# Early loads in the order of their use: a transformer block on one core, with its weight, halo and store transfers regrouped

## The chip, the cores and the metric

The kernel runs on one core of a Trainium2 chip. The metric is device time in microseconds of one execution. The core has a matrix engine (TensorE, PE in the profile; its weight loads are listed as PEld), a vector engine (VectorE, DVE), a scalar engine (ScalarE, ACT), GpSimd (POOL) and SyncE (SP), which here does nothing but issue DMA transfers. The transfers of all issuers run on the core's 16 DMA engines; q1 is the queue of SP, q10 that of ACT.

## The reference

The input `x` has 2048 tokens of D = 576 features, in bf16. Two branches are computed from the same layer norm of `x` and added to it:

```
xn  = layernorm(x)
A:  q, k, v = xn @ wqkv                  (32 heads of 18)
    each token attends to itself and 7 earlier ones, 2 apart
    (positions s, s-2, ... s-14; those before 0 are masked)
    a   = softmax(q.k / sqrt(18)) . v,   then a @ wo
B:  f   = (silu(xn @ w_gate) * (xn @ w_up)) @ w_down      (4608 hidden)
out = x + A + B
```

## The kernel before

**Layout.** Token s = 16 p + r stands in partition p as row r, so there are 16 "rows" of 128 tokens. The attention needs rows up to 14 back. A ring of 18 rows (`Kr`, `Vr`) holds the 14 last rows of the partition before (the halo, which must be moved across partitions by DMA) and four rows of its own.

**Buffers that serve twice.** `wd`, the down-projection weights, is 9 chunks of 576 KB. Before they are loaded, its first 62% hold the raw rows of x (`xc_b`, chunks 0 to 3) and the normalized rows (`xn_b`, in chunks 4 to 6). Chunks 7 and 8 hold nothing. `hT`, the hidden activations, holds in its front the QKV weights and in its second half four staging buffers (`stage`), two for keys and two for values, of four rows each. A group c of rows (4c to 4c + 3) uses key and value buffers 0 and 1 when c is even, 2 and 3 when c is odd, so row 8 writes over group 0 and row 12 over group 1.

**QKV stage, rows 0 to 15 in order (lines 456 to 481).** For each row r, PE computes q, k and v (`p_row0`, `p_row`, L268): five slices kt of the contraction, 432 columns at a time in four PSUM banks, 36 matmuls on half the partitions each from row 1 on. ACT copies the banks out (`p_evac`): q to `QO`, k and v to staging. Ahead of PE run layer norm on DVE and ACT (`ln_*`, `pair_stats`, `pair_apply`) and the transposition of the normalized row: on PE for rows 0 to 4 (L232, L250), by DMA from SP for rows 5 to 15 (`transp_dma`, L258). For rows 2 to 4 the PE transposes are put between the matmuls of the row before (`between`). PE's first matmuls are warm-up on zeros (`warm_pe`).

**Halos and stores (`halo`, L328).** Once group c is in staging, SP issues for keys and then for values: the halo in two pieces (112 and 15 partitions, L334 and L335), and the group itself, into the ring for group 0 (L337) or to DRAM for groups 1 to 3 (`kv_d`, L339), from where `ring_load` fetches it later.

**Feed-forward, four passes of four rows (line 521 on).** Each pass goes over 9 chunks of 512 hidden columns. `g_pair` makes gate and up with PE (L506), `g_evac` the product on ACT (L517, L518) and DVE (L519). Gate/up weights (`gu`, four transfers a chunk) have two slots: chunk i + 2 can be loaded into a slot once PE has read chunk i. Chunks 0 and 1 are loaded within the QKV stage (at rows 9 and 12). During pass 0, each chunk also loads one or two chunks of `wd` (order 8, 0, 1, ... 7) and a part of `wo`. Then the down and output projections follow for each row (L552, L555).

**Attention on DVE (`chain`).** Its steps stand in a list from which fixed points of the program take steps (`dve.take` in the QKV stage, `dve.pump` after each activation). Keys are multiplied at L364; offset 7 and 6 need halo group 1, 5 and 4 also group 2, 3 to 1 group 3.

**What sets the order.** Each engine, SP too, works through its own list strictly in the order of the program text; the schedule is written by hand. SP's list is one queue: a transfer is issued only after those in front of it have been, and one that waits holds all behind it. Transfers take eight completion semaphores in turn, so each also waits for the eighth one before it to have landed.

Of the kernel before, what the change touches and what calls it, by code (L numbers as in the profile page):

```python
# [29 lines left out]
R = 16  # L30
# [40 lines left out]
def kernel(  # L71
# [11 lines left out]
    nc = tc.nc  # L83
# [58 lines left out]
    def load_w(eng, kt):  # L142
        if kt < 4:
            eng.dma_start(wqkv[:, kt, :], A_wqkv[kt * P:(kt + 1) * P, :])
        else:
            for i in range(2):
                eng.dma_start(wqkvr[64 * i:64 * i + 64, :], A_wqkv[4 * P:D, 2 * G * i:2 * G * (i + 1)])

    nc.sync.dma_start(xc_b[0][0:64, 0, :], x_v[0:64, 0, :])
    nc.scalar.dma_start(xc_b[0][64:128, 0, :], x_v[64:128, 0, :])  # L150
    load_w(nc.scalar, 0)
    nc.sync.dma_start(xc_b[0][:, 1, :], x_v[:, 1, :])
    load_w(nc.scalar, 2)
    make_identity(nc, ident[:])
    load_w(nc.sync, 1)
    nc.sync.dma_start(xc_b[0][:, 2, :], x_v[:, 2, :])
    load_w(nc.sync, 3)
    load_w(nc.sync, 4)
    nc.sync.dma_start(xc_b[0][:, 3, :], x_v[:, 3, :])
    for c in range(1, 4):  # L160
        nc.sync.dma_start(xc_b[c], x_v[:, 4 * c:4 * c + 4, :])
    nc.scalar.activation(warm[:], eps_t[:], ACT.Sqrt)
# [38 lines left out]
    def ln_stats(r, n=1):  # L201
        c, j = divmod(r, 4)
        xc, xn, mv, rstd = ln[c]
        for i in range(j, j + n):
            stats = lns.tile([P, 2, 6], f32, name="stats")
            for k in range(2):
                nc.vector.bn_stats(stats[:, k, :], xc[:, i, k * HALF:(k + 1) * HALF])  # L207
            nc.vector.bn_aggr(mv[:, i, :], stats[:].rearrange("p c s -> p (c s)"))

    def ln_sqrt(r, n=1):  # L210
        c, j = divmod(r, 4)
        xc, xn, mv, rstd = ln[c]
        nc.scalar.activation(rstd[:, j:j + n], mv[:, j:j + n, 1], ACT.Sqrt, bias=eps_t[:], scale=1.0)

    def ln_recip(r, n=1):
        c, j = divmod(r, 4)
        rstd = ln[c][3]
        nc.vector.reciprocal(rstd[:, j:j + n], rstd[:, j:j + n])

    def ln_apply(r, lo=0, hi=D):  # L220
        c, j = divmod(r, 4)
        xc, xn, mv, rstd = ln[c]
        nc.vector.tensor_scalar(xn[:, j, lo:hi], xc[:, j, lo:hi], mv[:, j, 0:1], rstd[:, j:j + 1],
                                op0=ALU.subtract, op1=ALU.mult)
        if hi == D:
            nc.vector.tensor_copy(xn[:, j, D:DPAD], xn[:, j, 512:D])
# [64 lines left out]
    def p_row(r, between=None):  # L291


        t = [None] * NG
        fence = {}
        for swap in range(2):
            for i in range(2):
                kts = (0, 1, 2, 3) if swap else (0, 4, 1, 2, 3)
                for kt in kts:
                    for half in range(2):  # L300
                        g = i + 2 * (half ^ swap)
                        if t[g] is None:
                            t[g] = new_ps("qkv_ps")
                        mm = p_mm(t, g, kt, half, r, swap == 0 and kt == 0, swap == 1 and kt == 3)
                        if swap == 0 and kt == 3 and half == 1:
                            fence[i] = fence_after(mm)
                        if swap and kt == 0 and half == 0:
                            fence_before(mm, fence[i])
                if swap and i == 0 and between is not None:
                    between()  # L310
        return t

    def p_evac(r, t):
        c, j = divmod(r, 4)
        ks, vs = stage[2 * c % 4], stage[(2 * c + 1) % 4]
        vdst = vs[:, j, :].rearrange("p (d h) -> p d h", h=H)

        def v_copy(lo, n, src):
            nc.scalar.copy(vdst[:, :, lo:lo + n], src.rearrange("p (h d) -> p d h", d=DH))  # L319

        nc.scalar.copy(QO[:, r, 0:G], t[0][:, 0:G])  # L321
        nc.scalar.copy(ks[:, j, HALF:D], t[2][:, 0:HALF])
        v_copy(0, 8, t[2][:, HALF:G])
        nc.scalar.copy(QO[:, r, G:D], t[1][:, 0:D - G])
        nc.scalar.copy(ks[:, j, 0:HALF], t[1][:, D - G:G])
        v_copy(8, 24, t[3][:, 0:G])

    def halo(m, c):  # L328
        ring = Kr if m == 1 else Vr
        st = stage[(2 * c + m - 1) % 4]  # L330
        lo = 2 if c == 0 else 0
        s0 = 4 * c - 2 + lo
        n = 4 - lo
        nc.sync.dma_start(ring[1:113, s0:s0 + n, :], st[0:112, lo:4, :])  # L334
        nc.sync.dma_start(ring[113:128, s0:s0 + n, :], st[112:127, lo:4, :])  # L335
        if c == 0:
            nc.sync.dma_start(ring[:, HALO:HALO + RT, :], st)  # L337
        else:
            nc.sync.dma_start(kv_d[m - 1, c - 1], st.rearrange("p r d -> p (r d)"))  # L339

    def ring_load(m, tt):
        ring = Kr if m == 1 else Vr
# [85 lines left out]
    def first():  # L428
        pt = new_pt()
        transp_pe(1, range(KT), pt)  # L430
        ln_stats(2)
        copy_pt(nc.scalar.copy, 1, range(3), pt)
        copy_pt(nc.vector.tensor_copy, 1, range(3, KT), pt[:, 3 * P:])
        ln_sqrt(2)
        ln_recip(2)
        ln_apply(2)

    warm_pe(11)
    ln_open(0)
    ln_stats(0)  # L440
    ln_sqrt(0)
# [14 lines left out]
    for r in range(R):  # L456
        if r == 0:
            t = p_row0(first)
        else:
            t = p_row(r, (lambda: transp_halves(r + 1)) if r <= 3 else None)  # L460
        if r == 1:
            ln_recip(3)
            ln_apply(3)
        p_evac(r, t)
        if r == 0:
            ln_stats(3)
            ln_sqrt(3)
        if 2 <= r <= 7:
            pair_apply(2 * r)
        if 1 <= r <= 6:  # L470
            pair_stats(2 * r + 2)
        if r and r % 4 == 0 or r == R - 1:
            c = r // 4 - (r < R - 1)
            halo(1, c)
            halo(2, c)
        if r in (9, 12):
            load_gu((r - 9) // 3)
        if r == 7:
            chain(0)
        if r in (7, 8, 12):  # L480
            dve.take(3 if r == 7 else 6)


    wd_order = [8, 0, 1, 2, 3, 4, 5, 6, 7]
    wo_order = list(range(DH))
    ring_ps = {}

# [33 lines left out]
    for tt in range(NTT):  # L521
        for ch in range(NCH):
            it = tt * NCH + ch
            for p in range(2):
                g_pair(tt, ch, p)
                for j in (2 * p, 2 * p + 1):
                    g_evac(ch, j)
                    dve.pump(1.4)
                if 1 <= it <= 4:
                    for _ in range(3 if it <= 1 else 2):  # L530
                        load_wo(wo_order.pop(0))
            if ch == NCH - 1:
                dve.drain(lambda: chains[0] > tt)
                for r in range(RT * tt, RT * tt + RT):
                    nc.sync.dma_start_transpose(oT[:, :, r * P:(r + 1) * P], QO_t[:, r * D:r * D + KT * P])
            if it + NSLOT < NTT * NCH:
                load_gu(it + NSLOT)
            if tt == 0:
                for _ in range(2 if ch in (5, 6) else 1):
                    if wd_order:  # L540
                        load_wd(wd_order.pop(0))
            if ch == 4:
                nc.sync.dma_start(xr[:], x_v[:, RT * tt:RT * tt + RT, :])
            if ch == 1 and tt < NTT - 1:
                chain(tt + 1)
        for sub in range(RT):
            r = RT * tt + sub
            t = [new_ps("d_ps") for h in range(2)]
            for h in range(2):
                cols = slice(h * HALF, (h + 1) * HALF)  # L550
                for f in range(NF):
                    nc.tensor.matmul(t[h][:, 0:HALF], hT[:, f, sub * P:(sub + 1) * P], wd[:, f, cols],  # L552
                                     start=(f == 0), stop=False)
                for k in range(KT):
                    nc.tensor.matmul(t[h][:, 0:HALF], oT[:, k, r * P:(r + 1) * P], wo[:, k, cols],  # L555
                                     start=False, stop=(k == KT - 1))
            dve.pump(8.5)
            ot = tmp.tile([P, D], bf16, name="ot", tag="ot", bufs=3)
            for h in range(2):
                cols = slice(h * HALF, (h + 1) * HALF)  # L560
                nc.vector.tensor_tensor(ot[:, cols], t[h][:, 0:HALF], xr[:, sub, cols], op=ALU.add)  # L561
                if r == R - 1:
                    nc.sync.dma_start(out_v[:, r, cols], ot[:, cols])
            if r < R - 1:
                nc.sync.dma_start(out_v[:, r, :], ot[:])
# [30 lines left out]
```

## Time and profile before

| | us |
|---|---|
| median of 3 runs (lowest, highest) | 514.27 (512.72, 516.37) |
| profiled execution, its own time | 515.68 |
| its span | 513.8 |
| PE busy | 503.4 (98%) |
| DVE, ACT busy | 327.3, 199.8 |
| feed-forward pass 0, first to last matmul of L506 | 62.60 to 138.36 |
| pass 1, the same | 178.64 to 248.68 |

The times in views are microseconds from the start of the span. A wait "X <- Y" says that X stood idle until Y ended. Matmuls are pipelined and their ends are modelled, so "busy" for PE includes the time in which a matmul ran slowly; the granted clock (1.00 is full speed) stands in a column of its own. A DMA share of 1.00 means that all 16 DMA engines are moving bytes; it can come out a little above. The time to landing of a transfer is counted from its issue, and holds the time in which it stood behind others.

### The profile page before, as it was taken

To read this page: it belongs to the slowest core of one execution; us is meant where nothing else is said; L and a number is where in the kernel's file an instruction comes from. 1 tells how busy PE (TensorE), PEld (TensorE's weight loads), DVE (VectorE), ACT (ScalarE), POOL (GpSimd) and SP (SyncE) were. 2 spreads that over 40 slices of the span, in tenths; PEclk is the share of its full clock that TensorE was granted. 3 is DMA by queue.
4 is the path that set the end of the run, shared out by engine and by line. 5 is a ranking of instruction groups with operands and counts; after the bars stand their busy time and mean duration, and the time that the engine had idled before them with its cause. 6 is when DMAs were issued, how large, how long until landed. Compare 5 with 4: busy or idle time off the path is not lost.

```text
span 513.8 us, 10678 instructions
## 1 busy us (share of the span) xinstructions
PE 503.4 (98%) x4516; PEld 294.4 (57%) x4516; DVE 327.3 (64%) x472; ACT 199.8 (39%) x415; POOL 2.5 (0%) x10
## 2 busy tenths in 40 slices
PE   7999989999999999999999999999999999999997
PEld 3655755444577744444677644444777444445775
DVE  5784569798999969999797129996990122112010
ACT  3656644755500055554400255458000355454000
POOL 1000000000000000000000000000000000000000
PEclk9999989999999999999999999999999999999999
DMA  8379998889751036474622053654500145542000
GB/s 273 96 188 196 307 312 260 291 274 295 233 138 59 11 105 192 132 231 138 168 83 70 11 154 124 213 162 134 144 13 23 60 138 185 174 150 40 25 13 24
DMA packets 75711, 75.01 MB, mean 146 GB/s; under 512 B 21948, under 2 KB 71448, under 8 KB 75664
## 3 DMA queue, kind: packets, MB, share of 16 engines
q1 hardware_dynamic: 75232, 73.35, 47.5%
q10 hardware_dynamic: 368, 0.96, 0.6%
q8 instruction: 35, 0.57, 0.5%
q14 instruction: 12, 0.10, 0.1%
q0 software_dynamic: 64, 0.03, 0.0%
HBM read 58.69 MB, written 5.90 MB: 126 GB/s over the span
## 4 chain that ended last, share of the span: by engine, by line
PE 80%; DMA 6%; ACT 2%; SPq 1%; DVE 1%; issue 1%; ACTq 0%
PE g_ps L506 50%; PE d_ps L552 27%; PE d_ps L555 4%; DMA gu<-in_B_w_gate_dram 2%; DMA gu<-in_B_w_up_dram 2%; DMA kv_d<-hT 1%; SPq L335 1%; DMA xnT<-wd 0%; DVE ssum L390 0%; ACT uc L518 0%; ACT hT L319 0%; DVE hT L519 0%; SPq L178 0%; ACT L389 0%; DVE PP L396 0%
## 5 line engine op out<-in xcount | busy, mean ns | idle before, releaser
L506 PE MATMUL g_ps<-xnT,gu 64*128 64x512 bf16 x2592 | 283.2, 377 | 2.8 <-DMA gu<-in_B_w_up_dram 2.8
L506 PEld LDWEIGHTS <-gu 64*128 64x128 bf16 x2592 | 132.2, 94 | 152.8 <-DMA gu<-in_B_w_up_dram 4.2
L517 ACT ACTIVATE sg<-g_ps 128x512 bf16<-128x512 f32 x144 | 87.4, 607 | 163.6 <-PE g_ps L506 163.6
L552 PE MATMUL d_ps<-wd,hT 128*128 128x288 bf16 x1152 | 146.6, 286 | 0.5 <-DVE hT L519 0.5
L552 PEld LDWEIGHTS <-hT 128*128 128x128 bf16 x1152 | 112.4, 98 | 30.7 <-issue 1.3
L519 DVE TENSOR_TENSOR hT<-sg,uc 128x512 bf16<-128x512 bf16 x144 | 60.2, 418 | 93.3 <-ACT uc L518 93.3
L518 ACT CAST uc<-g_ps 128x512 bf16<-128x512 f32 x144 | 85.5, 594 | 0.0
L369 DVE TENSOR_REDUCE PP<-PP 128x64 f32<-128x1152 bf16 x64 | 85.0, 1346 | 0.5
L268 PE MATMUL qkv_ps<-hT,xnT 64*128 64x432 bf16 (+1 forms) x560 | 54.2, 343 | 1.6 <-DMA hT<-in_A_wqkv_dram 1.5
L364 DVE TENSOR_TENSOR PP<-QO,Kr 128x2304 bf16<-128x2304 bf16 (+1 forms) x35 | 43.5, 1249 | 16.5 <-DMA Kr<-hT 16.2
L561 DVE TENSOR_TENSOR ot<-d_ps,xr 128x288 bf16<-128x288 f32 x32 | 13.8, 452 | 58.7 <-PE d_ps L555 58.6
L268 PEld LDWEIGHTS <-xnT 64*128 64x128 bf16 (+1 forms) x560 | 31.5, 94 | 22.8 <-issue 2.4
L396 DVE TENSOR_TENSOR PP<-Vr,A 128x2304 bf16<-128x2304 bf16 (+1 forms) x35 | 43.3, 1250 | 0.5
L401 DVE TENSOR_TENSOR PP<-PP 128x2304 bf16<-128x2304 bf16 x24 | 32.5, 1354 | 0.4
L517 ACT ACT_TABLE_LOAD x5 | 6.4, 1283 | 52.4 <-PE g_ps L506 52.3
L555 PE MATMUL d_ps<-wo,xnT 128*128 128x288 bf16 x160 | 24.8, 286 | 0.0
L555 PEld LDWEIGHTS <-xnT 128*128 128x128 bf16 x160 | 15.6, 98 | 4.0
L319 ACT CAST hT<-qkv_ps 128x144 bf16<-128x144 f32 (+1 forms) x32 | 14.0, 439 | 2.7 <-DMA kv_d<-hT 2.7
L207 DVE BATCH_NORM_STATS2 stats<-wd 128x6 f32<-128x288 bf16 x32 | 12.7, 440 | 3.5 <-DMA wd<-in_A_x_dram 3.5
L389 ACT ACTIVATE PP<-PP 128x1024 f32<-128x1024 f32 x4 | 4.2, 1057 | 27.5 <-DVE PP L385 27.5
L321 ACT CAST QO<-qkv_ps 128x432 bf16<-128x432 f32 x16 | 8.3, 517 | 7.6 <-PE qkv_ps L268 7.5
L390 DVE TENSOR_REDUCE ssum<-PP 128x128 f32<-128x1024 f32 x4 | 7.6, 1912 | 2.3 <-ACT PP L389 2.3
(39 smaller groups left out, 89.3 us busy)
## 6 DMA issues: line engine op xcount, KB each, us to landing
gu<-in_B_w_gate_dram SPq DMA_DIRECT2D x36, 512.0 KB, 3.8
gu<-in_B_w_up_dram SPq DMA_DIRECT2D x36, 512.0 KB, 5.0
wd<-in_B_w_down_dram SPq DMA_DIRECT2D x9, 576.0 KB, 6.2
kv_d<-hT SPq DMA_DIRECT2D x6, 576.0 KB, 7.1
gu<-in_B_w_gate_dram SPq DMA_DIRECT2D x36, 64.0 KB, 4.7
gu<-in_B_w_up_dram SPq DMA_DIRECT2D x36, 64.0 KB, 4.4
xr<-in_A_x_dram SPq DMA_DIRECT2D x4, 576.0 KB, 5.7
out_dram<-ot SPq DMA_DIRECT2D x15, 144.0 KB, 1.8
```

Source lines behind the costliest of these rows:

```text
L268: return nc.tensor.matmul(t[g][:, 0:G], xnT[rows, kt, r * P:(r + 1) * P], w_at(g, kt, rows), start=start, stop=stop)
L319: nc.scalar.copy(vdst[:, :, lo:lo + n], src.rearrange("p (h d) -> p d h", d=DH))
L364: nc.vector.tensor_tensor(prod[:, a:b], QO[:, RT * tt + a:RT * tt + b, :], Kr[:, s:s + b - a, :], op=ALU.mult)
L369: nc.vector.tensor_reduce(L[:, w, rs], prod[:, rs].rearrange("p r (h d) -> p r h d", d=DH), axis=AX.X, op=ALU.add)
L396: nc.vector.tensor_tensor(dst[:, a:b], Vr[:, s:s + b - a, :].rearrange("p r (d h) -> p r d h", h=H), A[:, w, a:b].unsqueeze(2).to_broadcas ...
L401: nc.vector.tensor_tensor(dst, acc, pv, op=ALU.add)
L506: mm = nc.tensor.matmul(ring_ps[j][b][:], gu[rows, slot, k, fc], xnT[rows, kt, tok], start=(swap == 0 and kt == 0), stop=(swap == 1 and kt ...
L517: nc.scalar.activation(sg[:], t[0][:], ACT.Silu)
L518: nc.scalar.copy(uc[:], t[1][:])
L519: nc.vector.tensor_tensor(hT[:, ch * FC + j, :], sg[:], uc[:], op=ALU.mult)
L552: nc.tensor.matmul(t[h][:, 0:HALF], hT[:, f, sub * P:(sub + 1) * P], wd[:, f, cols], start=(f == 0), stop=False)
L555: nc.tensor.matmul(t[h][:, 0:HALF], oT[:, k, r * P:(r + 1) * P], wo[:, k, cols], start=False, stop=(k == KT - 1))
```

## The change

All is a matter of order; no arithmetic is changed.

- The QKV weight slices, two of which ACT issued, all go through SP, between the rows of x, in the order kt 0, kt 1, x row 1, kt 2, kt 3, x row 2, kt 4, x row 3.
- Gate/up chunk 0 and down chunk 7 are loaded at row 0, down chunk 8 at row 2, gate/up chunk 1 at row 8 ahead of the halos of group 1. Down chunks 0 to 6 follow in pass 0, one with each chunk.
- The key halo of group 0 goes out after row 4, the value halo after row 6. For groups 1 to 3, both halos go ahead of both stores, which are a function of their own (`store`). The stores of group 3 wait until after chunk 0 of pass 0, behind the load of gate/up chunk 2.
- The PE transposes of rows 2 to 4 are placed four matmuls earlier (after kt 1 of the second half's first bank pair, instead of after its kt 3).
- Layer norm of row 2: statistics after the copies of row 1's transposes, its square root on ACT after the first copy of row 0. Two more warm-up matmuls (13 for 11).

On SP the first rows of the list are now: x row 0 (half), the weights and x rows as above, x groups 1 to 3, gate/up chunk 0, down chunk 7, transpose of row 5, down chunk 8, transposes of rows 6 to 9, key halo of group 0, transposes of rows 10 to 13, value halo of group 0, transposes of rows 14 and 15, gate/up chunk 1, halos of group 1, stores of group 1, halos and stores of group 2, halos of group 3, gate/up chunk 2, stores of group 3, down chunk 0.

```diff
+    def load_x(j):
+        nc.sync.dma_start(xc_b[0][:, j, :], x_v[:, j, :])
+
     nc.sync.dma_start(xc_b[0][0:64, 0, :], x_v[0:64, 0, :])
     nc.scalar.dma_start(xc_b[0][64:128, 0, :], x_v[64:128, 0, :])
-    load_w(nc.scalar, 0)
-    nc.sync.dma_start(xc_b[0][:, 1, :], x_v[:, 1, :])
-    load_w(nc.scalar, 2)
     make_identity(nc, ident[:])
+    load_w(nc.sync, 0)
     load_w(nc.sync, 1)
-    nc.sync.dma_start(xc_b[0][:, 2, :], x_v[:, 2, :])
+    load_x(1)
+    load_w(nc.sync, 2)
     load_w(nc.sync, 3)
+    load_x(2)
     load_w(nc.sync, 4)
-    nc.sync.dma_start(xc_b[0][:, 3, :], x_v[:, 3, :])
+    load_x(3)
...
-                if swap and i == 0 and between is not None:
-                    between()
+                    if swap and i == 0 and kt == 1 and between is not None:
+                        between()
...
-    def p_evac(r, t):
+    def p_evac(r, t, between=None):
...
         nc.scalar.copy(QO[:, r, 0:G], t[0][:, 0:G])
+        if between is not None:
+            between()
...
-        else:
-            nc.sync.dma_start(kv_d[m - 1, c - 1], st.rearrange("p r d -> p (r d)"))
+
+    def store(m, c):
+        st = stage[(2 * c + m - 1) % 4]
+        nc.sync.dma_start(kv_d[m - 1, c - 1], st.rearrange("p r d -> p (r d)"))
...
         transp_pe(1, range(KT), pt)
-        ln_stats(2)
         copy_pt(nc.scalar.copy, 1, range(3), pt)
         copy_pt(nc.vector.tensor_copy, 1, range(3, KT), pt[:, 3 * P:])
-        ln_sqrt(2)
-        ln_recip(2)
-        ln_apply(2)
-
-    warm_pe(11)
+        ln_stats(2)
+
+    warm_pe(13)
...
-        p_evac(r, t)
         if r == 0:
+            p_evac(r, t, lambda: ln_sqrt(2))
+            ln_recip(2)
+            ln_apply(2)
             ln_stats(3)
             ln_sqrt(3)
+        else:
+            p_evac(r, t)
...
-        if r and r % 4 == 0 or r == R - 1:
-            c = r // 4 - (r < R - 1)
+        if r == 0:
+            load_gu(0)
+            load_wd(7)
+        if r == 2:
+            load_wd(8)
+        if r == 4:
+            halo(1, 0)
+        if r == 6:
+            halo(2, 0)
+        if r == 8:
+            load_gu(1)
+        if r in (8, 12, R - 1):
+            c = (r - 1) // 4 if r < R - 1 else 3
             halo(1, c)
             halo(2, c)
-        if r in (9, 12):
-            load_gu((r - 9) // 3)
+            if r < R - 1:
+                store(1, c)
+                store(2, c)
...
-    wd_order = [8, 0, 1, 2, 3, 4, 5, 6, 7]
...
             if tt == 0:
-                for _ in range(2 if ch in (5, 6) else 1):
-                    if wd_order:
-                        load_wd(wd_order.pop(0))
+                if ch == 0:
+                    store(1, 3)
+                    store(2, 3)
+                if ch < 7:
+                    load_wd(ch)
```

## The prediction, made before the result was known

> **What bounds the kernel now.** I read the engine shares first: PE is busy 503.4 of 513.8 us, so a shorter time can only come from PE's waits and from stretches in which it runs slowly. The chain that ended last shows where PE is late: it stands on the first feed-forward pass, and before it on DMAs.
>
> ```profile
> 49.26 6.42 DMA kv_d<-hT
> ...
> 63.10 10.23 DMA gu<-in_B_w_gate_dram
> ...
> 73.86 9.31 DMA gu<-in_B_w_up_dram
> ...
> 83.22 15.89 PE g_ps L506 x144
> ```
>
> Columns are start, length, what. The second gate/up chunk is 10 us on its way and the third 9 us, where a steady chunk's gate part lands in 3.8 us (the page's DMA issues). Then I cut the first pass at its chunk borders, for line 506 alone:
>
> ```profile
> 62.60:70.75 8.15, 8.15 (x73) 5.86 (x71) 1.00 1.07 316
> 70.75:73.00 2.25, 0.00 (x1) 0.01 (x1) 0.94 1.04 330
> 73.00:83.22 10.22, 9.67 (x72) 7.23 (x72) 0.85 0.93 294
> 83.22:91.20 7.98, 7.97 (x74) 3.63 (x76) 1.00 0.84 263
> ...
> 107.20:115.00 7.80, 7.80 (x76) 3.52 (x74) 1.00 0.88 283
> ```
>
> Columns: stretch, length, PE busy, weight-load busy, granted clock, DMA share, GB/s. A chunk should take 7.8 us (fifth line). The chain has whole passes at 70.04 us and the first at 138.36 - 62.60 = 75.76: **5.7 us too long**. It divides into 0.35 in the first chunk, 2.25 of waiting, 2.4 in the second chunk (0.55 waiting, the rest at a reduced clock) and 0.6 spread over later ones. All other passes and down projections repeat at their own length. So the kernel is 62.6 us of start and QKV, 5.7 of loss, and work that this change doesn't touch.
>
> Why are the chunks late? The DMA engines, in wider stretches over all engines (the last two figures are DMA share and GB/s):
>
> ```profile
> 16.00:21.50 5.50, 5.50 (x70) 3.31 (x68) 4.82 (x18) 3.97 (x14) 0.00 (x0) 1.00 0.01 3
> 21.50:30.00 8.50, 8.36 (x102) 4.45 (x100) 7.54 (x27) 4.67 (x16) 0.00 (x0) 1.00 0.52 81
> ...
> 40.00:46.00 6.00, 6.00 (x69) 3.19 (x67) 2.73 (x3) 3.26 (x11) 0.00 (x0) 1.00 0.66 129
> 46.00:62.00 16.00, 16.00 (x178) 10.63 (x176) 7.94 (x6) 9.25 (x30) 0.00 (x0) 1.00 1.00 299
> ```
>
> They idle for 5.5 us, run half empty until 30 and again before 46, and are then full until 84. The bytes fit into the time; they are in the wrong place.
>
> **Part 1: the early loads.** Chunk 0 (1.18 MB), down chunks 7 and 8 (0.59 MB each) go behind the x rows. Alone on the engines gate/up rows move at about 360 GB/s (63 to 67 us in the trace: 337 to 375), so chunk 0 and down chunk 7 take some 1.8 MB / 0.36 = 5.0 us, from 15.0 to 20.0, in the idle stretch. The first DMA transpose (row 5, L258) was issued at 20.61 and would now come near 19.7; it landed in 3.1 us at 23.7, and PE needs row 5 at about 25.4 before (row 4 begins near 22.1, a row is 3.28 us: the copies of L321 at 45.68, 48.97, 52.25) and 24.5 after (part 4). Margin 0.7 us after its landing at 23.7, and 1.6 if it moves with DVE, so I cost it at nothing. Chunk 8 (1.6 us) goes between the transposes of rows 5 and 6; the engines are 0.52 busy there. If that cover fails, see rival D.
>
> **Part 2: chunk 1 ahead of the second group of halos.** This is where the change can bite. SP issues in order, and was busy without a break from 29.25 to 44.8: a transpose, the first halos, six transposes of 1.23 to 2.11 us. The change only regroups these (value halos two rows later), so chunk 1 is issued at about 43.5, four issues of 2.3 us in all, and the key halo of rows 4 to 7 at about 46 (44.88 before). All four halo pieces now go ahead of both stores. Before, the value store landed at 49.26 + 6.4 = 55.7, and ScalarE stood for it, as staging of row 12 overwrites its source:
>
> ```profile
> ACT hT L319 <- DMA kv_d<-hT: 2.7, 1, 2.7
> ```
>
> PE paid nothing for that, but narrowly: row 12's first copy at 52.25 comes with 8 of 36 matmuls left, so row 12 ends near 53.0 and row 13 near 56.25, and the bank that row 14 then wants was free at 55.78 + 0.28 = 56.06. There are 0.2 us of slack. After: chunk 1 lands near 48 (3.1 us of bytes at 360 GB/s, and issue). In the full stretch from 56 to 68 the pieces landed one after the other: a halo 1.8 to 1.9 us apart, a store 1.4 to 2.1. So the value store lands at 48 + 3.7 + 2.8 to 4.2 = 54.5 to 55.9, and ScalarE frees the bank 0.3 later. Row 14 would begin at 55.35 (part 4). Stall: 0 to 0.85, I take 0.3, near the middle of these rows. The halos and stores of rows 8 to 11 find a queue without gate/up loads: key halo near 57.5 instead of 62.2.
>
> **Part 3: the first pass.** Both gate/up slots are full when it begins, so the waiting goes and with it the slow clock. What is late next: chunk 2 can only be issued when chunk 0 has been read, near 70.2. Ahead of it stand four halo pieces of rows 12 to 15, issued near 64 behind stores that end near 62: about 3.7 us, 68. The stores of rows 12 to 15 and down chunk 0 now queue behind that wait; the stores are due before chunk 6 writes over their staging, near 110, so nobody waits for them. It lands at 70.2 + 5, near 75.5, and is wanted at 62 + 15.6 = 77.6. DVE stood 16.2 us for key halos (L364, three waits) and now far less; its products for the first chunk end earlier, and four buffers of `sg` and `uc` cover the rest. The exponential of the first attention chain stays at its place and keeps about 0.3. Gain 5.72 - 0.3 = **5.4 us**; ends 4.5 (chunk 2 a little late) and 5.7.
>
> The price of a wait. At 70.75 PE stood for 2.25 us and the granted clock was then 0.50 from 73 to 76, and 1.9 us were lost to it. A wait of 1.3 us at 7.65 to 8.97 left it at 1.00. The Trainium skill ("TensorE: Matmul & The Clock Gate", Part 1) puts the loss of clock at an idle window of about 3.4 us; by that rule the second chunk would not have slowed, and only 3.5 us would be there to win. The row decides.
>
> **Part 4: the start.** Weight slices go in order of use on one queue. Before, PE had kt 0 at 6.75, then stood 1.32 us until 8.97 for kt 1 (SP's slice landed at 2.23 + 6.7, while ScalarE's queue took 24 to 87% of the engines from 2 to 6 us), and ended row 0 near 12.2. Kt 3 landed at 10.98, behind the slice of kt 1 and three transfers of x on SP's queue, was used at 11.04 for 0.7 us, and kt 4 (landed at 3.93 + 7.5 = 11.4) only at about 11.8. After, kt 0 to 3 come in turn, but kt 4 has the same 2.4 MB at the same rate ahead of it and lands at 11.2 to 11.4. So the wait for kt 1 goes and most of it returns at kt 4. Gain 0.3 to 0.9 (all of the 1.32 would need kt 4 by 10.9), I take 0.5. The transposes of rows 2 to 4, four matmuls earlier, hide their copy (PEld stood 1.3 us in three waits for it, which PE's pipeline mostly covered): 0 to 0.6, I take 0.4. Together row 14 begins 0.9 earlier, which DVE follows: it waited 1.8 us for row 2's transposes (L254). Two more warm-up matmuls are 0.4 to 0.8 us in a PE gap of 0.57 from 5.38: 0 to 0.25, I take 0. LN of row 2 reordered on DVE and ACT: nothing, DVE is ahead of PE there by that 1.8 us; 0.3 if not (one 0.29 us square root ahead of the copies of row 0).
>
> **Sum.** 0.9 - 0.3 + 5.4 = 6.0 us. The profiled execution took 515.68 (span 513.8 and 1.9 around it): 509.7. The median of the three runs is 514.27, 1.4 below, so **508.3 us**. About 1% (5.1 us) is what a measurement of this kernel can tell from no change; the three runs alone span 512.7 to 516.4.
>
> **Rivals.**
> A, the forecast, 506.5 to 510 by the ends above: 0.64.
> B, the stores land late. Chunk 1 goes at 250 GB/s (the rate of the chunk at 99 to 107 us) and lands near 49.7, the stores take 2.1 each: the value store near 57.7, the bank free at 58. PE stands 2.7 us, more than the 2.25 that cost the clock, so 1.9 more: 0.9 + 5.4 - 4.6 = 1.7 gained, 512.6. For it: chunk 1 is 1.18 MB in front of the stores, and slack was 0.2. Against: the half-idle stretch 40 to 46. Chance 0.17.
> C, the transfers stay as late as they were. The queue carries the same bytes to the third chunk; if the full stretch merely moves, chunk 2 lands near 80 and PE stands 2 us there, and the clock takes 1.9: 0.6 + 5.4 - 3.9 = 2.1, 512.2. Against: chunk 0 leaves the full stretch for the idle one, 4 to 5 us, and the last two stores go behind chunk 2, 3 more. Chance 0.11.
> D, slower: the DMA transposes. Beside ring copies one of them took 5.6 us to land and one issue 2.11, against 2.6 and 1.23. If streaming loads do that to rows 5 to 9, each lands 2.5 us later in a queue that is strictly in order, and five rows give 12 us of stall, with the clock twice 16: 6.3 - 16 = -9.7, 524. It decides when a transpose lands over 0.8 to 1.6 us later than now (the margin of part 1), and turns the sum once it costs over 6. Against: the loads are over by 20 to 22 us. Chance 0.08.
>
> **Numbers.** A gives 508.3. Of A some 0.84 lies below 509.1; B and C lie within 1%, D above. Faster 0.54, same 0.38, slower 0.08. The range takes A, C and B: 506 to 513.2; D and the edges, about 0.15, stay out.
>
> **What would show it.** Right: chunks 0 to 2 of the first pass at 7.8 to 8.0 us each with the clock at 1.00 throughout; no wait of PE for gate or up; DMA share near 1 from 15 to 20 us; the first feed-forward matmul at about 62.0. Wrong: a PE gap near 55 with a halved clock after it (B), a wait at the third chunk (C), `xnT<-wd` as a releaser of PE (D).

## The result, and the profile after

The changed kernel takes 516.31 us (median of 15 runs, 515.02 to 519.4); the kernel before, on the same chip, takes 514.31 (15 runs, 512.72 to 516.56). The ratio is **1.0043, 95% interval 1.0025 to 1.0061**: about 2 us slower, where 6 us of gain were forecast. 508.3 was predicted, with a range of 506 to 513.2; the result lies outside it.

The two profiled executions hide this: that of before took 515.68, 1.4 above its median, and that of after 515.02, 1.3 below its own and the shortest of the 15. Between the traces there is a gain of 0.66 us, between the medians a loss of 2.0, and 0.66 - 1.37 - 1.29 = -2.0 joins the two. What follows first is the trace; the experiments show which of its rows return.

PE is still the bound: the page has it busy 502.6 of 513.2 us. From the first matmul of the down projection to the last matmul 372.0 us pass in both traces (372.0 to 372.6 in all traces of this study), so all that differs between the two lies before that point. It came at 138.29 before and at 137.68 after, and the first feed-forward pass began at 62.60 before and at 63.91 after. QKV is thus 1.3 us longer and pass 0 is 1.9 us shorter (73.83 against 75.76, where 5.4 were expected).

The chain that ended last, of the kernel after (start, length, what; a length beside a DMA is its time from issue to landing):

```profile
39.30 3.61 DMA Vr<-hT
42.98 0.29 ACT hT L322
...
49.76 7.31 DMA kv_d<-hT
...
75.63 8.42 DMA wd<-in_B_w_down_dram
84.07 0.39 SPq L181
90.69 7.63 DMA gu<-in_B_w_up_dram
```

Gate/up chunks 1 and 2, which led this chain before, are gone from it. Three others are in it: the value halo of group 0 (`Vr<-hT` at 39.30, the last of its three transfers, which copies the group itself into the ring), a store (`kv_d<-hT` at 49.76), and gate/up chunks 3 and 4. The up part of chunk 3 SP could issue (84.07) only once a transfer of `wd` had landed. The first two are in the QKV stage. The groups of waits of the kernel after (us in total, times, longest) give their sizes:

```profile
ACT hT L322 <- DMA Vr<-hT: 3.5, 1, 3.5
ACT hT L327 <- DMA kv_d<-hT: 2.6, 1, 2.6
ACT hT L322 <- DMA kv_d<-hT: 1.0, 1, 1.0
PE qkv_ps L271 <- ACT hT L322: 1.4, 2, 0.9
PE g_ps L525 <- DMA gu<-in_B_w_up_dram: 2.4, 3, 2.0
```

ACT stands 3.5 us for the value halo at row 8, and PE behind it 0.5. ACT stands 2.6 us for the key store at row 12 and then 1.0 more for the value store, and PE behind it 0.9 at row 14. Pass 0, cut at its chunk borders, for line 525 alone (stretch, length, PE busy, weight-load busy, granted clock, DMA share, GB/s):

```profile
63.91:72.02 8.11, 8.11 (x75) 5.55 (x76) 1.00 0.50 144
72.02:79.80 7.78, 7.78 (x75) 5.30 (x72) 1.00 0.84 296
79.80:87.60 7.80, 7.80 (x73) 5.01 (x68) 1.00 0.76 229
87.60:89.63 2.03, 0.00 (x0) 0.01 (x1) 1.00 1.02 313
89.63:98.30 8.67, 8.33 (x72) 3.51 (x72) 1.00 0.96 287
```

Chunks 0 to 2 run as forecast, at 7.8 to 8.1 us and full clock. Then PE stands 2.03 us: the wait of 2.25 us at chunk 1 has become a wait of 2.03 at chunk 3. The DMA share says why this is not a lack of rate: the engines were 0.50, 0.84 and 0.76 busy while chunks 0 to 2 were computed. SP's list in that stretch (start, length, operation; x6 are six transfers in a row):

```profile
75.63 1.24 SPq L190 DMA_DIRECT2D wd<-in_B_w_down_dram  x1
76.92 4.52 SPq L187 DMA_DIRECT2D wo<-in_A_wo_dram  x6
82.58 0.39 SPq L180 DMA_DIRECT2D gu<-in_B_w_gate_dram  x1
84.07 0.39 SPq L181 DMA_DIRECT2D gu<-in_B_w_up_dram  x1
```

PE had read chunk 1 at 79.80, so its slot was free for chunk 3 from there. The gate part was issued at 82.58 and the up part at 84.07. Down chunk 0, issued at 75.63, landed 8.42 later at 84.05. The up part is the eighth transfer after it (six of `wo`, and the gate part, lie between), and needs its completion semaphore; SP's own waits in this stretch are 1.1 us for that (`SPq L181 <- DMA wd`), 1.1 of the gate part for a store of group 3, and 0.5 of `wo` for a store. The rest of the delay is issue time: the six of `wo` take SP 4.5 us, to 81.44 (the 0.5 included).

### The profile page after: what moved, and what is told of

It is laid out like the page before. It is cut to its first block, busy times and chain, and to the rows that moved or that the text cites. A ratio compares the mean times of both kernels' runs of the same rounds, so it can differ in the third digit from the quotient of the medians.

```text
span 513.2 us, 10683 instructions
## 1 busy us (share of the span) xinstructions
PE 502.6 (98%) x4518; PEld 296.1 (58%) x4518; DVE 327.8 (64%) x472; ACT 200.1 (39%) x415; POOL 2.5 (0%) x10
## 4 chain that ended last, share of the span: by engine, by line
PE 82%; DMA 7%; DVE 5%; SPq 3%; ACT 2%; issue 1%; ACTq 0%
PE g_ps L525 48%; PE d_ps L573 27%; PE d_ps L576 4%; PE qkv_ps L271 3%; DMA wd<-in_B_w_down_dram 2%; DMA gu<-in_B_w_up_dram 1%; DMA kv_d<-hT 1%; DVE stats L210 1%; DMA hT<-in_A_wqkv_dram 1%; DVE wd L226 1%; DMA Vr<-hT 1%; SPq L187 1%; SPq L144 0%; DVE mv L211 0%; DVE ssum L397 0%
## 5 line engine op out<-in xcount | busy, mean ns | idle before, releaser
L271 PEld LDWEIGHTS <-xnT 64*128 64x128 bf16 (+1 forms) x560 | 32.9, 94 | 23.1 <-issue 4.5
## 6 DMA issues: line engine op xcount, KB each, us to landing
gu<-in_B_w_gate_dram SPq DMA_DIRECT2D x36, 512.0 KB, 3.7
gu<-in_B_w_up_dram SPq DMA_DIRECT2D x36, 512.0 KB, 5.1
```

Of the source, the lines that this page charges most:

```text
L271: return nc.tensor.matmul(t[g][:, 0:G], xnT[rows, kt, r * P:(r + 1) * P], w_at(g, kt, rows), start=start, stop=stop)
```

## The experiments

My theory after the result: the change loses in two places in QKV, where a transfer out of a staging buffer goes out later and ACT, then PE, stands for the buffer; and what it wins at chunks 1 and 2 it gives back at chunk 3, because SP's list holds chunk 3's load back. Rivals: that the difference is the clock of single executions and not order; that chunk 3 is late for want of bytes per second; that the new order at the start costs time.

One table holds what every trace showed. "Pass 0" is the first matmul of the feed-forward, "down" the first of the down projection. The first four experiments ran on one chip, the next four on a second, the last four on a third, each beside runs of the kernel before there (medians 514.55, 513.71, 514.06).

| kernel | pass 0 | down | length | median | ratio to before, 95% |
|---|---|---|---|---|---|
| before | 62.60 | 138.29 | 75.7 | 514.31 | |
| after | 63.91 | 137.68 | 73.8 | 516.31 | 1.0043 [1.0025, 1.0061] |
| again | 65.06 | 138.76 | 73.7 | 516.63 | 1.0045 [1.0026, 1.0064] |
| vhalo4 | 66.28 | 139.30 | 73.0 | 518.74 | 1.0081 [1.0054, 1.0108] |
| gu1late | 63.26 | 137.87 | 74.6 | 515.41 | 1.0023 [1.0002, 1.0044] |
| both | 62.41 | 136.11 | 73.7 | 513.66 | 0.9984 [0.9965, 1.0003] |
| both_wo | 62.21 | 132.24 | 70.0 | 510.41 | 0.9926 [0.9903, 0.9949] |
| both_st | 61.77 | 133.62 | 71.9 | 510.72 | 0.9926 [0.9906, 0.9947] |
| both_wo_st | 62.30 | 134.61 | 72.3 | 511.81 | 0.9946 [0.9925, 0.9968] |
| startonly | 63.05 | 137.76 | 74.7 | 514.25 | 1.0004 [0.9986, 1.0023] |
| chg_wo | 65.69 | 136.27 | 70.6 | 513.59 | 0.9992 [0.9969, 1.0015] |
| bef_wo | 62.47 | 134.96 | 72.5 | 513.82 | 0.9986 [0.9959, 1.0014] |
| early | 62.50 | 134.26 | 71.8 | 511.81 | 0.9956 [0.9935, 0.9978] |
| early_wo | 62.20 | 133.06 | 70.9 | 510.54 | 0.9936 [0.9910, 0.9962] |

### again: the changed kernel unaltered

> The changed kernel, unaltered. Its profile on record (515.0 us) is the fastest of 15 executions, and before's (515.7) lies above its median, so the two traces understate the loss by some 2.6 us. Theory 1 (the waits are the same, but a wait near 2 us halves the PE clock in some executions and not in others): time 516.3, and this trace has again a wait of ScalarE for the value halo near 43 us (3.5), one for a store near 57 (3.6) and one of PE for chunk 3 near 88 (2.0), now with a clock below 1.00 after one of them, about 1.5 us longer. Theory 2 (the loss is elsewhere, spread over the passes): the passes 1 to 3 are longer than 70.04 us.

The ratio repeats (1.0045), and so do the waits, in another execution: 3.5 us of ACT for the value halo, 3.1 and 1.0 for the stores, 1.37 of PE at row 14 (0.88 in the first trace), 1.73 at chunk 3 and 0.80 at chunk 4. Pass 0 begins at 65.06, 1.15 later than in the first trace; row 0 was 0.7 of that. This execution took 516.12, close to the median, and the clock was 1.00 from row 8 to the end of pass 0; the reduced clock that I had expected in it was not there. So the loss doesn't need a reduced clock, and the first trace was a lucky one up to pass 0.

### vhalo4: the value halo of group 0 back to its old place

```diff
         if r == 4:
             halo(1, 0)
-        if r == 6:
             halo(2, 0)
```

> The value halo of group 0 goes out after row 4 again, behind the key halo; all else as changed. Theory A (two waits in a row on one queue; the later one, row 12 for the stores, is set by SP's queue and not by PE): ScalarE's 3.5 us for the value halo and PE's 1.0 us at row 10 are gone, but row 14 then waits 2.1 instead of 1.1, the first feed-forward matmul stays at 63.9 and the time at 516.3 (within 0.4). Theory B (the waits are independent): feed-forward begins at 62.9, time 515.3.

The wait for `Vr<-hT` is gone, and the kernel is slower still: 518.74, where 516.3 or 515.3 was expected. PE's instructions of the QKV stage (start, length, in brackets the idle time before it and what ended it), and two stretches of 1 us of the same trace over all engines (the last three figures are granted clock, DMA share, GB/s):

```profile
58.19 8.41 PE L271 MATMUL qkv_ps<-hT,xnT 64*128 64x432 bf16 x71 [2.90 <-ACT hT L322]
```

```profile
58.00:59.00 1.00, 0.81 (x6) 0.48 (x7) 0.96 (x2) 1.00 (x5) 0.00 (x0) 0.66 1.03 221
59.00:60.00 1.00, 1.00 (x8) 0.53 (x6) 1.00 (x2) 1.00 (x6) 0.00 (x0) 0.50 1.08 272
```

What the early stall had cost was moved to the later one, and more: rows run on time to row 12, ACT then stands 4.7 us for the store instead of 2.6, and PE 2.90 at row 14. After that wait the granted clock is 0.50 and rows 14 and 15 take 8.41 us where they took 6.73, another 1.7. The two stalls are one after the other on one path. PE comes to row 14 1.3 us earlier than in the first trace (0.7 of it because row 0 was earlier), and is released 0.7 later; together that is the 2.0 us by which its wait grew. The profiled execution took 516.69, 2.0 below the median, so the median holds more than this trace shows: three of the nine executions have a mean clock of 0.990 to 0.993, this one has 0.997.

### gu1late: chunk 1 behind the halos and stores of group 1

```diff
-        if r == 8:
-            load_gu(1)
...
                 store(1, c)
                 store(2, c)
+        if r == 8:
+            load_gu(1)
```

> Gate/up chunk 1 is issued behind the halos and stores of group 1; all else as changed. Theory A: the stores of group 1 land some 4 us earlier, ScalarE's 3.6 us for them at row 12 and PE's 1.1 at row 14 go, feed-forward begins at 62.8; time 515.2. Chunk 1 lands before 62, early enough. Rival: the stores are slow for themselves (7 us each), and row 12 still waits over 2 us: 516.3.

The waits for stores are gone; the 3.5 us of ACT for the value halo stay, with 0.48 of PE. 515.41 us, 1.2 less than again (medians; the intervals of the two ratios overlap, by about half), where 515.2 was expected. Pass 0 begins at 63.26. So chunk 1 ahead of the halos and stores is what delays the stores.

### both: the two edits together

> Both: value halo after row 4, chunk 1 behind the stores of group 1. Theory A: both PE stalls of the QKV stage go, 2.1 us, feed-forward begins near 61.8 and the time is 514.2, that of before; the wait for chunk 3 stays at about 2.0. Theory B: the same sum. If feed-forward begins early and the time still stays over 515.5, the loss is in pass 0 and not in the QKV stage.

No stall of PE is left in QKV; pass 0 begins at 62.41, and the time is 513.66, 3.0 below again. That is the price of the two moves of the halos and chunk 1, and it closes the first half of the theory. The second half stays. PE's instructions in the feed-forward of this kernel, and SP's:

```profile
87.83 8.20 PE L524 MATMUL g_ps<-xnT,gu 64*128 64x512 bf16 x72 [1.73 <-DMA gu<-in_B_w_up_dram]
96.76 39.42 PE L524 MATMUL g_ps<-xnT,gu 64*128 64x512 bf16 x359 [0.73 <-DMA gu<-in_B_w_up_dram]
```

```profile
74.02 1.23 SPq L190 DMA_DIRECT2D wd<-in_B_w_down_dram  x1
75.29 4.13 SPq L187 DMA_DIRECT2D wo<-in_A_wo_dram  x6
80.63 0.39 SPq L180 DMA_DIRECT2D gu<-in_B_w_gate_dram  x1
82.37 0.38 SPq L181 DMA_DIRECT2D gu<-in_B_w_up_dram  x1
```

Chunk 1 had been read near 62.41 + 15.7 = 78.1, and its slot's next load went out 2.5 and 4.3 us later. With QKV repaired, the whole change is worth 0.16%, not distinguishable from nothing.

### both_wo: and the output weights three chunks later

The 18 transfers of `wo` (36 KB each, six of them in a row at first) go with chunks 4 to 7 instead of 1 to 4; nothing else of SP's list moves.

```diff
-                if 1 <= it <= 4:
-                    for _ in range(3 if it <= 1 else 2):
+                if 4 <= it <= 7:
+                    for _ in range(3 if it <= 4 else 2):
```

> As the run with both halo edits, and the loads of the output weights (18 transfers of 36 KB) at chunks 4 to 7 of pass 0 instead of 1 to 4, so that chunk 3's load follows down chunk 0 on SP. Semaphore theory: chunk 3's load was held on SP until the eighth transfer before it had landed (store, down chunk 0); without six small transfers in between its eighth one before belongs to chunk 2 and it is issued when chunk 1 is read, near 78.4 instead of 82 to 84. Its bytes still stand behind two stores and down chunk 0, so it lands near 86.5 and PE's 1.7 us wait at chunk 3 shrinks to 0.5; chunk 4's 0.7 goes. Time 512.0. Byte theory: the bytes ahead alone set the landing, wait and time as before this edit: 513.7.

510.41 us, 0.64% below the before of its chip by the medians and 0.74% by the ratio, where both was at 0.16%: some 3 us, and 512.0 was expected. PE's line for pass 0 is now a single one, without a wait, and 70.0 us from first to last is the length of the later passes (70.04 in the chain). SP's list beside it:

```profile
62.21 70.09 PE L524 MATMUL g_ps<-xnT,gu 64*128 64x512 bf16 x648
```

```profile
73.81 1.15 SPq L190 DMA_DIRECT2D wd<-in_B_w_down_dram  x1
77.95 0.38 SPq L180 DMA_DIRECT2D gu<-in_B_w_gate_dram  x1
78.38 0.51 SPq L181 DMA_DIRECT2D gu<-in_B_w_up_dram  x1
```

Chunk 3's load goes out the moment its slot is free, 0.4 us between gate and up. What was moved in front of it are six transfers of 36 KB, 0.22 MB: at the 300 GB/s of this stretch 0.7 us. Its issue came 2.7 to 4.0 us earlier. So it is their number, as issues of SP and in the turn of the semaphores, and not their own bytes, that held chunk 3. How much each of the two has was not tried; in the trace of both SP is done with the six at 79.42, 1.3 us after chunk 1 had been read, and then waits 1.1 us for a store before the gate part and 1.3 for down chunk 0 before the up part. They do not hold a load at every place: in both_wo the same six stand in front of chunk 6 (96.28 to 100.10), and its gate part goes out at 101.26, one chunk's length of 7.8 us after that of chunk 5 (93.49).

### both_st: instead, the stores of group 3 later

```diff
-                if ch == 0:
+                if ch == 3:
                     store(1, 3)
                     store(2, 3)
```

> As the run with both halo edits, and the two stores of group 3 (0.59 MB each) behind chunk 5's load instead of chunk 2's (in chunk 3 of pass 0). Both theories: down chunk 0 lands near 79 instead of 82.4, chunk 3's load is issued near 80 and lands near 84.5, before chunk 2 ends at 85.9: no wait at chunk 3. Byte theory: the two stores make chunk 5 or 6 late by the same amount instead, time 513.5. Otherwise the engines' spare share there (0.84 with 1.00 as full) takes them up and the time is 511.5.

The two stores stand between chunk 2's load and down chunk 0; taken out, everything behind them in the list comes sooner. The wait at chunk 3 is gone, and a smaller one, 0.48, is left at chunk 6. 510.72, where 511.5 or 513.5 was expected: as good as both_wo within the intervals. So of the two things ahead of chunk 3, moving either is enough.

### both_wo_st: all of them

> As both halo edits, with output weights and the stores of group 3 both later. If pass 0's loss is all waiting for its chunks, all chunks take 7.8 us and pass 0 is 70.5 us: time 510.5. If something else keeps chunks long, no better than the better one of the two alone.

511.81, above each alone by 1.1 and 1.4, where 510.5 was expected. The intervals of the ratios overlap, but five of the six executions are slower than every one of both_st. The stores and `wo` were put into the same chunks, 3 and 4, and pile up again there: two stores, a down chunk and six of `wo` take SP from 95.75 to 102.0, the gate part behind them was issued at 102.60 and its up part at 104.82 (101.26 and 101.70 in both_wo). PE waits 0.56 at chunk 6 (behind ACT) and 0.54 at chunk 7 (for up weights). Here two good moves that share a place were not worth the sum of the two.

### startonly: the kernel before with only the new start

Queue order of weight slices and x rows, transposes four matmuls earlier, layer norm of row 2 reordered, 13 warm-up matmuls; nothing else.

> The kernel before with the start of the changed one alone: one queue for weights and x rows, earlier transposes, two more warm-up matmuls, layer norm of row 2 reordered; halos, stores and all later loads as before. The first copy of row 0 came at 12.26 before and at 11.9, 12.6, 12.4, 12.4 and 11.3 in five traces with this start. Theory 1: the start is worth 0.1 us on the mean, and what it gives is lost at row 14, which waits for the stores of group 1 (0.2 us of slack): time 514.5, unchanged within 0.5. Theory 2 (as forecast): 0.6 to 0.9 faster, 513.8.

1.0004 [0.9986, 1.0023]: no gain; the interval allows 0.7 us of it at the most. The first copy of row 0 came at 12.98 in this trace, against 12.26 before. Over the other nine traces with the new start it lies between 11.26 and 12.64, over the four with the old one between 11.89 and 12.26, and the means, this trace included, are 12.1 and 12.1; the spread of the executions is larger than any effect of order on it. One small gain does return: from the first copy of row 1 to that of row 4, the rows with the moved transposes, it takes 10.65 to 10.67 us in all ten traces with the new start and 10.85 or 10.86 in the four with the old one. The trace also shows what the change would have had to cure, and the clock after it:

```profile
80.99 56.84 PE L512 MATMUL g_ps<-xnT,gu 64*128 64x512 bf16 x503 [2.02 <-DMA gu<-in_B_w_up_dram]
```

Chunk 2 is late by 2.02 us here, chunk 1 is not late. The granted clock is 0.50 from 82 to 85. So which chunk is late in the old order, and by how much, differs between executions.

### chg_wo, bef_wo: the output weights later, alone

> The changed kernel with one edit: the output weights at chunks 4 to 7 of pass 0. The QKV stage keeps both its stalls (value halo, stores), so feed-forward begins at 64 to 65 as in its two traces. If the order on SP is the one cause of pass 0's loss there, pass 0 takes 70.1 us instead of 73.8, as in the run with both halo edits: 516.5 - 3.7 = 512.8. If the loss had two causes (order on SP, and late halos), over 515.

> The kernel before with the same one edit. Its PE waits for chunk 1 (2.25 us) and chunk 2 (0.55), and both were on their way before the first output-weight transfer is issued. Theory: what the edit frees begins at chunk 3, which there is not late, so the waits stay and the time is 514.0 (within 0.7). Rival: the small transfers are the cause in both kernels, 511.

In the changed kernel the edit makes pass 0 70.6 us long without a wait for a chunk, as in both_wo:

```profile
44.46 21.55 PE L271 MATMUL qkv_ps<-hT,xnT 64*128 64x432 bf16 x215 [1.88 <-ACT hT L322]
65.69 70.65 PE L525 MATMUL g_ps<-xnT,gu 64*128 64x512 bf16 x648
```

It gives 513.59, 0.9992 of before, where 512.8 was expected. The QKV stalls are still there, and in this execution the one for the value halo reached 4.8 us of ACT and 1.88 of PE, and took the clock with it. In the kernel before, the same edit isn't worth a measurable amount (0.9986 [0.9959, 1.0014]): its gate/up chunks 1 and 2 are loaded ahead of `wo`, and only 0.98 us at chunk 2 were lost in that trace.

### early, early_wo: only the early loads

`early` is the kernel before, its halos, stores and start untouched; only gate/up chunk 0 and down chunks 7 and 8 go early, and gate/up chunk 1 at row 9 behind the stores.

```diff
-        if r in (9, 12):
-            load_gu((r - 9) // 3)
+        if r == 0:
+            load_gu(0)
+            load_wd(7)
+        if r == 2:
+            load_wd(8)
+        if r == 9:
+            load_gu(1)
...
-    wd_order = [8, 0, 1, 2, 3, 4, 5, 6, 7]
+    wd_order = [0, 1, 2, 3, 4, 5, 6]
...
-                for _ in range(2 if ch in (5, 6) else 1):
+                for _ in range(1):
```

> The kernel before with the early loads alone: chunk 0 and down chunk 7 at row 0, down chunk 8 at row 2, chunk 1 at row 9 (behind the halos and stores of group 1, where chunk 0 was). Start, halos, stores and their order as before. Theory: the QKV stage ends as before (62.6), no wait at chunk 1, so the clock is not lost; chunk 2 comes a little late (behind the group's last stores), and chunk 3 is held by the small transfers as in the changed kernel: 513.5, a gain of 0.7. If early loads alone were enough: 509 to 510.

> The early loads alone and the output weights at chunks 4 to 7, halos and stores as in the kernel before. Theory: pass 0 is 70.1 to 71, a gain of 3 to 5 over before: 510.3, as good as the changed kernel with three edits (510.4 on its chip), so that the regrouping of halos and stores and the new start are worth nothing. Rival: the interleaved stores make chunk 2 late by 1 to 2 us, 512.

511.81, a ratio of 0.9956 [0.9935, 0.9978], where 513.5 was expected, and with `wo` later 510.54, 0.9936 [0.9910, 0.9962], where 510.3 was expected. The lines of PE in pass 0, of early:

```profile
78.83 16.20 PE L511 MATMUL g_ps<-xnT,gu 64*128 64x512 bf16 x145 [0.42 <-DMA gu<-in_B_w_up_dram]
95.30 39.03 PE L511 MATMUL g_ps<-xnT,gu 64*128 64x512 bf16 x358 [0.26 <-DMA gu<-in_B_w_gate_dram]
```

and of early_wo, again one without a wait:

```profile
62.20 70.93 PE L511 MATMUL g_ps<-xnT,gu 64*128 64x512 bf16 x648
```

The early loads are thus a gain of 0.44% by themselves, and the rest of the change (halos and stores regrouped, stores of group 3 held back, new start) turned it into a loss of 0.43%. early_wo, both_wo and both_st, the fastest three, beat both kernels, and the intervals don't tell them apart: no gain of the regrouped halos and stores is seen even where they do no harm.

One expectation failed here: that chunk 3 would be held as in the changed kernel. SP's rows for it in early:

```profile
79.68 0.39 SPq L177 DMA_DIRECT2D gu<-in_B_w_gate_dram  x1
81.11 0.38 SPq L178 DMA_DIRECT2D gu<-in_B_w_up_dram  x1
```

The six of `wo` stand in front of chunk 3 here too, and its parts go out some 1.5 and 2.9 us after chunk 1 had been read (62.50 + 15.7 = 78.2). But the stores of group 3 have gone out before chunk 2's load, chunk 3 lands sooner, and PE, which chunk 2 kept 0.8 us, just doesn't stand for it (the large up part landed at 86.6 and chunk 3 began then; without that delay PE would have come to it at 62.50 + 3 x 7.77 = 85.8). The move of `wo` is worth 1.3 us here between the medians (the intervals overlap) and some 3 in the changed order. So `wo` alone would make chunk 3 late by some 0.8 us, an estimate from these times; the 2 us of the changed kernel came from `wo` behind the two stores that the change held back.

## Why the prediction was wrong

**Part 1, the early loads: right.** They cost PE nothing (early begins pass 0 at 62.50, before at 62.60) and fill the idle stretch. Two stretches of the kernel after, over all engines:

```profile
16.00:21.50 5.50, 5.50 (x79) 5.40 (x76) 5.00 (x18) 3.71 (x13) 0.00 (x0) 1.00 0.94 274
21.50:30.00 8.50, 8.50 (x103) 4.82 (x99) 7.35 (x27) 5.10 (x18) 0.00 (x0) 1.00 0.79 164
```

The engines idled at 0.01 from 16 to 21.5 before, now they are 0.94 busy. The first DMA transpose was issued at 20.18 and landed 3.3 us later, against the 3.1 of before. The second, with down chunk 8 on its way beside it, took 3.2 to 5.1 us in the eleven traces with early loads and 2.6 in the three without. So what rival D feared, a transpose 2.5 us later, did happen to one row in some traces, but PE had the margin: no transpose by DMA is a releaser of PE, and rows 4 to 8 take 12.74 or 12.75 us in all fourteen. Rival D's stall, the only one on the slower side, did not occur, and the loss came from where no rival of mine stood.

**Part 2, first failed step: "The change only regroups these (value halos two rows later)".** This was written of SP's list, and priced at nothing. I had looked at when SP is free, not at who waits for the source of the transfer. The value halo of group 0 reads a staging buffer that row 8 writes over. Issued after row 6 (37.57 to 39.84) behind four more transposes, it landed at 42.9, and ACT could not write before. The line of ACT in the kernel after:

```profile
42.98 0.28 ACT L322 CAST hT<-qkv_ps 128x144 bf16<-128x144 f32 x1 [3.48 <-DMA Vr<-hT]
```

PE's share was a wait of 0.5 and 0.8 us of delay at row 10 in this trace (7.4 us from the first copy of row 8 to that of row 10, 6.6 before); in chg_wo 1.88 and a halved clock. The rule that I had used for stores ("staging of row 12 overwrites its source") holds for row 8 and the halo in the same way.

**Part 2, second step, mis-sized: the stall at row 14, "0 to 0.85, I take 0.3".** The mechanism was right, as rival B had it. The term that was off is the landing of chunk 1: the last of its four parts landed at 49.3, not near 48, close to the 49.7 of rival B. The value store landed at 49.76 + 7.31 = 57.07, where 54.5 to 55.9 was forecast and 57.7 by rival B; the 7.8 us between the two lie within the 3.7 + 2.8 to 4.2 of the forecast. PE lost 1.0 us from row 12 to 15 in this trace (first copies 10.91 apart, 9.89 before), and its wait alone was 1.37 in again. Rival B's price of 2.7 was too high here, as the first stall had already put PE back, and near to the 2.90 of vhalo4, where nothing had delayed the rows before. The two steps together cost 3.0 us between medians (again to both).

**Part 3, the main step: "Gain 5.72 - 0.3 = 5.4".** Chunks 0 to 2 came out nearly as written, chunk 2 with little to spare: issued from 72.03, it had landed at 78.8, 6.7 us later where 5 was forecast, and PE wanted it at 79.5. It failed at "What is late next": I followed the queue to chunk 2 and stopped. For the stores of group 3, which the change holds back behind chunk 2's load, I wrote "nobody waits for them". Nobody waits for their data, but chunk 3's load waits for their semaphore, with `wo` between. Rival C had a wait of 2 us of the right size, one chunk too early and for another reason (bytes). It was the order of the list: the wait goes with 0.22 MB of `wo` moved from in front of chunk 3 (both_wo), or with the two stores moved (both_st), and either time the kernel gains some 3 us; in early, where the stores are not held back, chunk 3 is hardly late even with `wo` in front.

**Part 3, second step: the 1.9 us of clock were counted as if each execution lost them.** I priced the gain from one execution of before (515.68), which held a wait of 2.25 us and a halved clock behind it, and then took the 1.4 us between it and the median off as well. The traces of startonly and bef_wo, with the same halos, stores and gate/up loads as before, lost 2.02 and 0.98 us at chunk 2 and had pass 0 at 74.7 and 72.5 us instead of 75.7. About the pass 0 that I forecast (75.76 - 5.4 = 70.4) was in the end measured (70.0, both_wo), and the whole gain with it is 0.74%, 3.8 us (3.3 between the medians), not 6.0. How often before loses the clock its other executions show: of the 83 beside the experiments 33 have a mean granted clock of 0.995 to 0.997, like the profiled one with 0.996, and a median of 515.4 us; the other 50 have 0.999 or 1.000 and 513.6. So the price was nearly right, 1.8 us, but only some four executions in ten pay it.

**Part 4, the start: 0.9 forecast, nothing measured.** The wait for kt 1 did return, though not at kt 4 alone as argued, but at kt 1, 2 and 4 (0.21, 0.63 and 0.34 us in the trace after), and the end of row 0 was not earlier by a measurable amount: startonly is at 1.0004. Of the 0.4 for the earlier PE transposes 0.2 is there (10.66 for 10.85 us from row 1 to row 4), too little for the medians to show. The ends that I gave, "0.3 to 0.9" and "0 to 0.6", left out that a sum of waits removed at one point may return whole.

The sum in the terms of the forecast, for the traces: 0.9 became -1.3 with the -0.3 (pass 0 begins 1.31 later), 5.4 became 1.9. For the medians: 2.0 lost. Undone, the two moves in QKV give back 3.0 and the order of `wo` another 3, which leaves some 4 as what the early loads win in an undisturbed list; the 3.3 to 3.8 of both_wo and the 3.5 of early_wo (514.06 to 510.54) are that size.

## What to carry to other kernels

A transfer that is moved later has two kinds of waiters: those who need what it writes, and those who want to write over what it reads; list both for every moved transfer, halos included. When a wait at chunk n is removed, follow the queue's list on until a chunk is in time with room to spare: what stands between two large loads here cost by the number of transfers, their issue time and their turn at a semaphore, and not by bytes alone. Price a gain from the median's loss, not from the loss in one profiled execution: a row that shows a halved clock may be an event of that execution, as in 33 of the 83 here.

## What was not expected of the hardware

**The clock falls after waits of about 2 us, but not always.** The granted clock was 0.50 for 3.4 us each time, beginning between 0.3 us before the end of the wait and 0.9 after it, when PE had waited 1.88 us (chg_wo), 2.02 (startonly), 2.21 (gu1late), 2.25 (before) and 2.90 (vhalo4). It stayed at 1.00 after 2.03 us (after) and 1.73 (again, both). Half of 3.4 is 1.7 us, and 1.7 to 1.9 is what rows 14 and 15 of vhalo4 and the second chunk of before lost, so a wait near 2 us may cost twice what its row says, or not, in the same kernel. The Trainium skill ("TensorE: Matmul & The Clock Gate", Part 1) puts the loss after an idle window of about 3.4 us and says that the window runs freely, so that its phase differs between runs; the second part would fit a wait of 2.03 without and one of 1.88 with a loss, but the length doesn't fit: five waits shorter than 3 us lost the clock here, and the measurement decides.

**Streaming loads slowed one DMA transpose in some executions and hardly in others.** The one issued next after down chunk 8's load landed 3.2 to 5.1 us later in eleven traces, 2.6 in the three without that load; the slow ones of before (up to 5.6 us to landing) had stood beside ring copies.
